# Attention stage: earlier loads, another order on ScalarE, eleven units of maxima, and products on quarters of the array

## The chip, the cores and the metric

The kernel runs on one core of one Trainium2 chip. The metric is device time in microseconds, from the start to the end of one execution, as a median of runs. Of the engines, PE is TensorE's matrix multiplication, PEld its loading of weights, DVE is VectorE, ACT ScalarE, POOL GpSimd and SP SyncE, which here issues the DMAs.

## What is computed

Pooled attention over 4 batches of 8 heads, and behind it two dense layers with a gate. The change touches the attention alone.

```
def _attn_ref(q, k, v):                      # (4, 8, 1152, 64) each, float32
    q_pool = q.reshape(B, H, S // 2, 2, D).mean(axis=3)
    scores = np.matmul(q_pool, k.transpose(0, 1, 3, 2)) / np.sqrt(D)
    scores = scores - np.max(scores, axis=-1, keepdims=True)
    attn = np.exp(scores)
    attn = attn / (np.sum(attn, axis=-1, keepdims=True) + 1e-09)
    return np.matmul(attn, v)

x = attn_out as (2304, 512)
x = (h - tanh(h)) @ w_out            with h = x @ w_in        # first layer
x = (h * sigmoid(1.702 h)) @ w_out   with h = x @ w_in        # second layer
```

## The kernel before

**Stages.** A short preparation, the attention, then the two layers (`moe`). The attention goes by pairs of heads: 16 pairs `p`, one head on partitions 0 to 63 and the other on 64 to 127 (`sides`). A pair has 576 pooled queries (`SP`) and 1,152 keys. It is worked in two halves `x` of 288 queries (`HB`), each over nine tiles of 128 keys: 18 steps `g` per pair, grouped three by three into six *bursts* `c` = 0 to 5. The main loop runs over 96 bursts. Its order is written out by hand, and each engine works through its own instructions in that order; so does SP through its DMAs.

**A burst** issues three times `scores` (L344: four products per head that split q and k into a high and a low part and add the row of maxima; then L347, the exponential on ACT into one of eight buffers `pf`), the units of maxima for the next pair, the additions of probabilities, three times `pv` (L356, v's product, whose two heads lie on the two column halves of the array), and after these a list of `jobs`. `scores` and units share three PSUM slots (`ps`); `acc` and `sm` have one bank each.

**Maxima.** The softmax needs each row's maximum before a pair's scores. `unit` multiplies high parts alone (L292, L300) and DVE reduces the product (L305). There are 14 units per pair: twelve of 2 x 384 columns and two of 2 x 288 for the last 64 queries (the corner). They run in the bursts of the pair before, as 2, 2, 3, 2, 3 in bursts 1 to 5, and the two corners in burst 0 of the pair itself. `max_rows` combines them in two parts, transposes on DVE (L321) and writes rows with six and four small DMAs (L327).

**Sums.** The probabilities are added by two chains: two of three on POOL, the third on DVE (L376). In the next burst 0 or 3 `merge` adds the chains on DVE (L381), and `total` multiplies by ones (L388) and copies to `us` on ACT (L390). `sums` moves one row per head to 128 partitions (L396), `recip` adds the epsilon on POOL (L402), inverts on DVE (L404) and writes to DRAM (L406), `spread` reads it back to all partitions (L412), `normalise` multiplies on DVE (L421).

**Preparation of later pairs.** q and k load at burst 3 of two pairs ahead (L244, L249), k's high part is copied in bursts 4 and 5 on ACT (L277), q's pairs are added on DVE in burst 5 (`qs`, L260), `qh` is copied on ACT in burst 0 (L264), the low parts are subtracted on DVE (L271) and POOL (L284). The loop also loads eight pieces of the layers' weights (L114) and converts each in five steps (L127 to L156), in pairs 3, 4, 6, 7, 9, 10, 12 and 13: the load in burst 0, and one step in each of bursts 1 to 5.

Of the kernel before, what the change touches and what calls it, by code (L numbers as in the profile page):

```python
# [28 lines left out]
def tile_pooled_attention_two_moe(  # L29
# [172 lines left out]
    def attention(ctx: ExitStack):  # L202
# [3 lines left out]
        sides = slice(0, 64), slice(64, 128)  # L206
        KN = S // 3
        QL = SP - 4 * 128
# [8 lines left out]
        sel = ap.tile([128, 128], F32R, name="sel")  # L217
        ones = ap.tile([128, 64], F32, name="ones")
        mts = [[fixed(f"{nm}{i}", 32) for nm in ("mt", "m2", "m3")] for i in range(2)]
# [35 lines left out]
        def have(p, nm, *args):  # L255
            return pairs[p].get(nm) or new(p, nm, *args)

        def prep_qs(p, x=slice(0, SP), eng=nc.vector):
            qs = have(p, "qs", SP, F32, 1)
            eng.tensor_add(qs[:, x], qraw[p][:, 0, x], qraw[p][:, 1, x])  # L260
# [25 lines left out]
        def unit(p, n):  # L286
            d = pairs[p]
            mx = ps.tile([128, 2, 512], F32, tag="ps", name="mx")
            if n < 12:
                j, c = divmod(n, 3)  # L290
                for s, r in enumerate(sides):
                    nc.tensor.matmul(  # L292
                        mx[:, s, 0:KN], d["qh"][r, 128 * j:128 * j + 128],
                        d["kh"][r, KN * c:KN * c + KN], start=True, stop=True)
                at, w = 8 * c + 2 * j, KN
            else:
                a, w = n - 12, HB
# [6 lines left out]
                at = 24 + 2 * a  # L304
            nc.vector.tensor_reduce(  # L305
                d["mt"][:, at:at + 2], mx[:, :, 0:w], AX.X, ALU.max, negate=True)

# [42 lines left out]
        def pv(g):  # L350
            p, i = divmod(g, 2 * KT)
            x, t = divmod(i, KT)
            if t == 0:
                accs[p, x] = ps_acc.tile([128, 512], F32, tag="acc", name="acc")[:, 0:HB]
            for s, r in enumerate(sides):
                nc.tensor.matmul(  # L356
                    accs[p, x][r], pairs[p]["v"][:, s, t, :], probs[g][:, s, :],
                    start=(t == 0), stop=(t == KT - 1))

# [18 lines left out]

        def merge(p, x):
            one, two = parts.pop((p, x, 0))[0], parts[p, x, 1][0]  # L380
            nc.vector.tensor_add(two, two, one)  # L381

        def total(p, x, *more):
            sm = ps_acc.tile([128, 512], F32, tag="sm", name="sm")[:, 0:HB]
            terms = [parts.pop((p, x, 1))[0], *more]
            for n, m in enumerate(terms):
                for s, r in enumerate(sides):
                    nc.tensor.matmul(  # L388
                        sm[r], ones, m[:, s, :], start=(n == 0), stop=(n == len(terms) - 1))
            nc.scalar.activation(results[p][1][:, HB * x:HB * x + HB], sm, AF.Copy)  # L390

        def sums(p):
            us = results[p][1]
            s9 = wpool.tile([128, QJ], F32, tag="s9", name="s9", bufs=2)
            for s, r in enumerate(sides):
                nc.sync.dma_start(  # L396
                    out=s9[r], in_=us[64 * s:64 * s + 1, :].rearrange("o (p i) -> o p i", i=QJ))
            norm[p] = dict(s9=s9)

        def recip(p):  # L400
            r9 = wpool.tile([128, QJ], F32, tag="r9", name="r9", bufs=2)
            nc.gpsimd.tensor_scalar(  # L402
                out=r9, in0=norm[p]["s9"], scalar1=1.0, scalar2=1e-9, op0=ALU.mult, op1=ALU.add)
            nc.vector.reciprocal(r9, r9)  # L404
            rd = drpool.tile([128, QJ], F32, tag="rd", name="rd", bufs=2)
            nc.sync.dma_start(out=rd, in_=r9)  # L406
            norm[p]["rd"] = rd
# [5 lines left out]

        def normalise(p):
            b, hp = divmod(p, NPB)
            t0, done = b * SP, 0
            while done < SP:
                blk = max(x for x in range(NB) if T0S[x] <= t0 + done)
                o = t0 + done - T0S[blk]
                n = min(TBS[blk] - o, SP - done)  # L420
                nc.vector.tensor_mul(  # L421
                    xb[blk][:, hp, o:o + n], results[p][0][:, done:done + n], rbd[:, done:done + n])
                done += n

        NC = 6
        jobs = {}

        def at(p, c, fn, *args):
            jobs.setdefault((p, c), []).append(lambda: fn(*args))

        units = {(0, 0): [(0, 9), (0, 10), (0, 11)], (0, 1): [(0, 12), (0, 13)]}
        for p in range(1, NPAIR):
            n = 0
            for c, m in enumerate((1, 3, 3, 2, 3) if p == 1 else (2, 2, 3, 2, 3), 1):
                units.setdefault((p - 1, c), []).extend((p, n + i) for i in range(m))
                n += m
            units.setdefault((p, 0), []).extend([(p, 12), (p, 13)])
        assert sum(len(u) for u in units.values()) == 14 * NPAIR - 9

        order = (("i", 0), ("i", 1), ("o", 0), ("i", 2), ("i", 3), ("o", 1), ("o", 2), ("o", 3))  # L440
        for p, (kind, f) in zip((3, 4, 6, 7, 9, 10, 12, 13), order, strict=True):
            for c, job in enumerate(piece(kind, f)):
                at(p, c, job)
        for c in range(NKC):
            at(NPAIR - 2 + c // 2, 2 * (c % 2) + 1, split_x, 0, [c], nc.gpsimd)

        for p in range(NPAIR):
            if p > 0:
                at(p - 1, 0, load_v, p)
                at(p - 1, 0, prep_kl, p, 0)  # L450
                at(p - 1, 1, prep_corner, p)
                at(p - 1, 2, prep_ql, p)
                at(p - 1, 3, prep_kl, p, 1)
                at(p, 1, sums, p - 1)
                at(p, 2, recip, p - 1)
                at(p, 3, spread, p - 1)
                at(p, 5, normalise, p - 1)
            if p > 1:
                at(p - 2, 3, load_q, p)
                at(p - 2, 3, load_k, p)  # L460
                at(p - 2, 4, new_pair, p)
                at(p - 2, 4, prep_kh, p, 0)
                at(p - 2, 5, prep_kh, p, 1)
                at(p - 2, 5, prep_qs, p)
                at(p - 1, 0, prep_qh, p)

# [34 lines left out]
        prep_qh(1)  # L501
        for n in range(9):
            unit(0, n)
            keep_warm(3)
        max_rows(0, 0)
        keep_warm(15)

        for c in range(NC * NPAIR):
            p, c = divmod(c, NC)
            x, part = divmod(c, 3)  # L510
            g = p * 2 * KT + 3 * c
            todo = units.get((p, c), [])
            before = (p, 0) if x else (p - 1, 1)
            closing = (p, c) == (NPAIR - 1, NC - 1)
            scores(g)
            for u in todo[:1]:
                unit(*u)
            if part == 0 and before[0] >= 0:
                merge(*before)
            scores(g + 1)  # L520
            scores(g + 2)
            for u in todo[1:]:
                unit(*u)
            if c == 4 and p + 1 < NPAIR:
                max_rows(p + 1, 0)
            if (p, c) == (0, 1) or p > 0 and c == 0:
                max_rows(p, 1)
            if closing:
                merge(p, x)
                add(p, x, 1, 6)  # L530
                add(p, x, 1, 7)
            else:
                for t in (0, 1):
                    add(p, x, 0, 3 * part + t)
# [7 lines left out]
            for job in jobs.pop((p, c), ()):  # L542
                job()
        total(NPAIR - 1, 1, probs[2 * KT * NPAIR - 1])
        sums(NPAIR - 1)
        assert not jobs
        return (lambda: recip(NPAIR - 1), lambda: spread(NPAIR - 1), lambda: normalise(NPAIR - 1))

# [237 lines left out]
```

## Time and profile before

| | us |
|---|---|
| median of 3 runs | 1310.68 (1302.87 to 1314.27) |
| the profiled execution | 1308.84 |
| its span, first to last instruction | 1307.1 |
| PE busy in it | 1236.5 (95%) |
| DVE busy | 974.4 (75%) |
| ACT busy | 633.8 (48%) |
| POOL busy | 475.1 (36%) |

A busy share is an average over the attention and the layers. PE's busy time counts an instruction until its modelled end, so products that overlap leave no gap even where the array streams only part of the time. The starts of instructions are what to compare. A wait is the idle time of an engine ahead of an instruction, put down to whatever released it last.

### The profile page before, as it was taken

To read this page: it belongs to the slowest core of one execution; us is meant where nothing else is said; L and a number is where in the kernel's file an instruction comes from. 1 tells how busy PE (TensorE), PEld (TensorE's weight loads), DVE (VectorE), ACT (ScalarE), POOL (GpSimd) and SP (SyncE) were. 2 spreads that over 40 slices of the span, in tenths; PEclk is the share of its full clock that TensorE was granted. 3 is DMA by queue.
4 is the path that set the end of the run, shared out by engine and by line. 5 is a ranking of instruction groups with operands and counts; after the bars stand their busy time and mean duration, and the time that the engine had idled before them with its cause. 6 is when DMAs were issued, how large, how long until landed. Compare 5 with 4: busy or idle time off the path is not lost.

```text
span 1307.1 us, 20184 instructions
## 1 busy us (share of the span) xinstructions
PE 1236.5 (95%) x7950; PEld 984.5 (75%) x7950; DVE 974.4 (75%) x1190; ACT 633.8 (48%) x944; POOL 475.1 (36%) x329
## 2 busy tenths in 40 slices
PE   8998798888888799999999999999999999999998
PEld 6665555555555567889879889889889889889887
DVE  5877787878888775999999999999943645645433
ACT  3554455444544455777665665665543322322211
POOL 5665565666666664223332332332200100100000
PEclk9999999999999999999999999999999999999999
DMA  3122222212222210111111111101211111111012
GB/s 117 58 101 80 73 74 81 82 65 81 81 65 81 81 29 11 58 36 62 49 33 49 49 33 37 46 33 49 65 33 49 49 33 49 49 33 33 25 41 80
DMA packets 27934, 72.82 MB, mean 56 GB/s; under 512 B 8640, under 2 KB 9152, under 8 KB 27840
## 3 DMA queue, kind: packets, MB, share of 16 engines
q1 hardware_dynamic: 27840, 71.54, 16.7%
q8 instruction: 62, 1.02, 0.3%
q14 instruction: 32, 0.26, 0.1%
HBM read 66.58 MB, written 4.79 MB: 55 GB/s over the span
## 4 chain that ended last, share of the span: by engine, by line
PE 52%; DVE 23%; ACT 8%; DMA 8%; issue 5%; SPq 3%; POOL 1%; DVEq 0%; ACTq 0%; POOLq 0%
PE y L670 21%; PE h L575 20%; PE sc L344 4%; PE acc L356 4%; DVE mt L305 4%; DMA kr<-in_k_dram 3%; DVE gg L633 3%; DVE gg L616 2%; SPq L327 2%; DVE s L376 2%; ACT u L614 2%; ACT pf L347 2%; DVE wt L134 2%; ACT a L635 1%; PE mx L292 1%
## 5 line engine op out<-in xcount | busy, mean ns | idle before, releaser
L305 DVE TENSOR_REDUCE mt<-mx 128x2 fp32r<-128x768 f32 (+1 forms) x224 | 203.4, 923 | 80.2 <-PE mx L292 77.9
L376 POOL TENSOR_TENSOR s<-s,pf 128x576 f32<-128x576 f32 x126 | 179.5, 1425 | 120.2 <-ACT pf L347 115.0
L347 ACT ACTIVATE pf<-sc 128x576 f32<-128x576 f32 x288 | 181.7, 649 | 73.7 <-PE sc L344 70.4
L575 PE MATMUL h<-hl,big 128*128 128x512 f32 (+1 forms) x940 | 211.6, 377 | 0.0
L575 PEld LDWEIGHTS h<-hl,big 128*128 128x128 f32 x940 | 174.0, 188 | 28.5
L156 POOL TENSOR_TENSOR big<-wt,big 128x512 fp32r<-128x512 f32 x46 | 61.5, 1336 | 365.3 <-ACT big L155 365.3
L670 PE MATMUL y<-g,big 128*128 128x512 f32 (+1 forms) x780 | 185.1, 368 | 0.7 <-POOL g L587 0.6
L670 PE MATMUL y<-big,g 128*128 128x512 f32 x702 | 181.0, 390 | 0.0
L356 PE MATMUL acc<-pf,v 128*64 128x288 f32 x1152 | 167.4, 428 | 0.0
L670 PEld LDWEIGHTS y<-g,big 128*128 128x128 f32 x780 | 142.7, 188 | 20.4 <-POOL g L587 1.9
L670 PEld LDWEIGHTS y<-big,g 128*128 128x128 f32 x702 | 131.6, 188 | 27.1
L585 ACT ACTIVATE g<-gg 128x1024 fp32r<-128x1024 f32 (+1 forms) x80 | 78.0, 974 | 137.9 <-DVE gg L646 78.2
L344 PE MATMUL sc<-qh,kh 64*128 64x288 f32 x576 | 104.1, 357 | 35.0 <-ACT pf L347 30.6
L690 DVE TENSOR_TENSOR xb<-xb,y 128x512 f32<-128x512 f32 (+1 forms) x114 | 72.1, 654 | 86.8 <-PE y L670 86.8
L575 PE MATMUL h<-hl,w 128*128 128x512 f32 (+1 forms) x564 | 127.0, 377 | 0.0
L344 PEld LDWEIGHTS sc<-qh,kh 64*128 64x128 f32 x576 | 54.6, 185 | 95.3 <-ACT pf L347 52.8
L356 PEld LDWEIGHTS acc<-pf,v 128*64 128x64 f32 x1152 | 76.3, 141 | 61.5 <-issue 23.9
L575 PEld LDWEIGHTS h<-hl,w 128*128 128x128 f32 x564 | 104.4, 188 | 17.1
L587 POOL TENSOR_TENSOR g<-gg,g 128x1024 fp32r<-128x1024 f32 (+1 forms) x39 | 87.1, 2234 | 65.2 <-ACT g L585 65.2
L635 ACT ACTIVATE a<-u 128x1024 f32<-128x1024 f32 (+1 forms) x40 | 39.1, 977 | 132.0 <-DVE gg L633 132.0
L642 ACT ACTIVATE a<-h 128x1024 f32<-128x1024 f32 (+1 forms) x40 | 37.6, 941 | 117.5 <-PE h L575 117.5
L344 PE MATMUL sc<-row,sel 64*128 64x288 f32 x576 | 86.4, 293 | 1.6 <-issue 1.4
(88 smaller groups left out, 2081.5 us busy)
## 6 DMA issues: line engine op xcount, KB each, us to landing
raw<-in_moe_w_in_dram SPq DMA_DIRECT2D x32, 512.0 KB
raw<-in_moe_w_out_dram SPq DMA_DIRECT2D x32, 512.0 KB
v<-in_v_dram SPq DMA_DIRECT2D x16, 576.0 KB
kr<-in_k_dram SPq DMA_DIRECT2D x15, 576.0 KB
qr<-in_q_dram SPq DMA_DIRECT2D x15, 576.0 KB
rbd<-rd SPq DMA_DIRECT2D x32, 144.0 KB
out_dram<-xb SPq DMA_DIRECT2D x18, 256.0 KB
row<-tt SPq DMA_DIRECT2D x128, 0.5 KB
```

The costliest lines, as they stand in the source:

```text
L156: nc.gpsimd.tensor_tensor(lo, t, f32(hi), op=ALU.subtract)
L305: nc.vector.tensor_reduce(d["mt"][:, at:at + 2], mx[:, :, 0:w], AX.X, ALU.max, negate=True)
L344: nc.tensor.matmul(sc[:, s, 0:HB], w[r], m[r, xs], start=(n == 0), stop=(n == 3))
L347: nc.scalar.activation(pf, sc[:, :, 0:HB], AF.Exp, scale=SCALE)
L356: nc.tensor.matmul(accs[p, x][r], pairs[p]["v"][:, s, t, :], probs[g][:, s, :], start=(t == 0), stop=(t == KT - 1))
L376: eng.tensor_add(out, old, new)
L575: nc.tensor.matmul(hb[:, j, 0:TBS[b]], wi[:, c, w, :], x[r][c], start=(k == 0), stop=(k == 3 * NKC - 1))
L585: nc.scalar.activation(gt[:, :, 0, :], g, AF.Copy)
L587: eng.tensor_tensor(gt[:, :, 1, :], g, f32(gt[:, :, 0, :]), op=ALU.subtract)
L635: nc.scalar.activation(a, u, AF.Relu, bias=-T2)
L670: nc.tensor.matmul(ys[m][:, 0:w], lhsT, rhs, start=(fp == 0 and not low and j == p == 0), stop=(fp == 1 and low and j == 1))
L690: nc.vector.tensor_add(dst, dst, ys[m][:, 0:w])
```

## The change

- The units become eleven: eight of 2 x 512 columns, one (n = 6) that takes the last 128 columns of four query tiles at once, and the two corners. In bursts 1 to 5 they are 2, 2, 2, 1, 2. The first unit of a burst goes behind its second scores.
- `jobs` can be marked `pre`: these are issued ahead of the burst's additions and of v's product, the others behind them as before. The copies `kh`, `qh`, the corner, and the first and last step of a weight piece are `pre`.
- q and k load at burst 0 (two pairs ahead); `qs` is added on POOL at burst 4, in two buffers.
- `pv` and `total` issue four products of 32 output columns, each on its own quarter of the array. `merge` goes: `total` gives the sum of POOL's chain and that of DVE's chain on different quarters, `sums` moves four rows instead of two, and `recip` adds the two and the epsilon in one DVE instruction.
- `normalise` is done in two pieces, one at burst 4 and one at burst 0 of the next pair.
- A weight piece is spread over two pairs, its load in burst 5 ahead of them. `split_x` of the first block goes to pair 15 and from POOL to DVE.

```diff
-        KN = S // 3
+        KN = S - 2 * 512
-            qs = have(p, "qs", SP, F32, 1)
+            qs = have(p, "qs", SP, F32, 2)
 def unit(p, n):
-            if n < 12:
-                j, c = divmod(n, 3)
+            if n == 6:
+                for j in range(4):
+                    for s, r in enumerate(sides):
+                        nc.tensor.matmul(
+                            mx[:, s, KN * j:KN * j + KN], d["qh"][r, 128 * j:128 * j + 128],
+                            d["kh"][r, 2 * 512:], start=True, stop=True)
+                out = d["mt"][:, 16:24].rearrange("p (j s) -> p j s", j=4)
+                src = mx.rearrange("p s (j k) -> p j s k", j=4)
+            elif n < 9:
+                j, c = divmod(n if n < 6 else n - 1, 2)
...
+            nc.vector.tensor_reduce(out, src, AX.X, ALU.max, negate=True)
 def pv(g):
-            for s, r in enumerate(sides):
+            for n in range(4):
+                s, h = divmod(n, 2)
                 nc.tensor.matmul(
-                    accs[p, x][r], pairs[p]["v"][:, s, t, :], probs[g][:, s, :],
-                    start=(t == 0), stop=(t == KT - 1))
+                    accs[p, x][32 * n:32 * n + 32], pairs[p]["v"][:, s, t, 32 * h:32 * h + 32],
+                    probs[g][:, s, :], start=(t == 0), stop=(t == KT - 1))
-        def merge(p, x):
-            one, two = parts.pop((p, x, 0))[0], parts[p, x, 1][0]
-            nc.vector.tensor_add(two, two, one)
 def total(p, x):
+            for n in range(4):
+                s, h = divmod(n, 2)
+                nc.tensor.matmul(
+                    sm[32 * n:32 * n + 32], ones, parts[p, x, h][0][:, s, :], start=True, stop=True)
 def sums(p):
+            for n in range(4):
+                s, h = divmod(n, 2)
                 nc.sync.dma_start(
-                    out=s9[r], in_=us[64 * s:64 * s + 1, :].rearrange("o (p i) -> o p i", i=QJ))
+                    out=s9[sides[s], h, :],
+                    in_=us[32 * n:32 * n + 1, :].rearrange("o (p i) -> o p i", i=QJ))
 def recip(p):
-            nc.gpsimd.tensor_scalar(
-                out=r9, in0=norm[p]["s9"], scalar1=1.0, scalar2=1e-9, op0=ALU.mult, op1=ALU.add)
+            nc.vector.scalar_tensor_tensor(
+                out=r9, in0=s9[:, 0], scalar=1e-9, in1=s9[:, 1], op0=ALU.add, op1=ALU.add)
 the jobs
-        for p, (kind, f) in zip((3, 4, 6, 7, 9, 10, 12, 13), order, strict=True):
+            p = 2 * n + 2
+            when = ((p - 1, 5), (p, 0), (p, 3), (p + 1, 0), (p + 1, 3), (p + 1, 4))
...
+                at(*w, job, pre=n in (1, 5))
-            at(NPAIR - 2 + c // 2, 2 * (c % 2) + 1, split_x, 0, [c], nc.gpsimd)
+            at(NPAIR - 1, 1 + c, split_x, 0, [c], nc.vector)
-                at(p - 1, 1, prep_corner, p)
-                at(p - 1, 2, prep_ql, p)
+                at(p - 1, 1, prep_corner, p, pre=True)
+                at(p - 1, 3, prep_ql, p)
-                at(p, 5, normalise, p - 1)
+                at(p, 4, normalise, p - 1, (0,))
+                if p + 1 < NPAIR:
+                    at(p + 1, 0, normalise, p - 1, (1,))
-                at(p - 2, 3, load_q, p)
-                at(p - 2, 3, load_k, p)
-                at(p - 2, 4, new_pair, p)
-                at(p - 2, 4, prep_kh, p, 0)
-                at(p - 2, 5, prep_kh, p, 1)
-                at(p - 2, 5, prep_qs, p)
-                at(p - 1, 0, prep_qh, p)
+                at(p - 2, 0, load_q, p)
+                at(p - 2, 0, load_k, p)
+                at(p - 2, 4, new_pair, p, pre=True)
+                at(p - 2, 4, prep_kh, p, 0, pre=True)
+                at(p - 2, 5, prep_kh, p, 1, pre=True)
+                at(p - 2, 4, prep_qs, p, slice(0, SP), nc.gpsimd)
+                at(p - 1, 0, prep_qh, p, pre=True)
 the main loop
             scores(g)
+            scores(g + 1)
             for u in todo[:1]:
                 unit(*u)
-            if part == 0 and before[0] >= 0:
-                merge(*before)
-            scores(g + 1)
             scores(g + 2)
             for u in todo[1:]:
                 unit(*u)
+            for job in jobs.pop((p, c, True), ()):
+                job()
...
         total(NPAIR - 1, 1)
```

## Rows read from the trace of the kernel before

**Rows 1.** Windows by pairs: stretch, us, busy PE, PEld, DVE, ACT, POOL; sums over 14, 5, 8
```profile
20.20:46.70 26.50, 26.16 (x264) 17.91 (x262) 20.68 (x30) 14.13 (x25) 17.41 (x12) 1.00 0.18 65
...
482.30:505.50 23.20, 20.95 (x220) 14.16 (x216) 11.73 (x16) 12.68 (x23) 14.90 (x12) 1.00 0.07 15
...
sum 435.60, PE 378.32 PEld 251.31 DVE 350.12 ACT 214.47 POOL 273.68; mean PE 27.02 PEld 17.95 DVE 25.01 ACT 15.32 POOL 19.55
...
sum 146.60, PE 131.41 PEld 87.15 DVE 119.14 ACT 73.51 POOL 100.45; mean PE 26.28 PEld 17.43 DVE 23.83 ACT 14.70 POOL 20.09
...
sum 260.30, PE 220.76 PEld 146.59 DVE 207.74 ACT 126.22 POOL 154.91; mean PE 27.60 PEld 18.32 DVE 25.97 ACT 15.78 POOL 19.36
```

**Rows 2.** Waits in the fourteen inner pairs: who waited for whom, us, times, longest
```profile
PEld sc L344 <- ACT pf L347: 50.9, 70, 3.4
...
ACT kh L277 <- DMA kr<-in_k_dram: 22.9, 13, 3.0
ACT wa L127 <- DMA raw<-in_moe_w_in_dram: 15.2, 4, 4.5
PEld mx L300 <- DVE mt L305: 14.1, 13, 1.4
ACT wa L127 <- DMA raw<-in_moe_w_out_dram: 12.7, 4, 3.6
PEld mx L292 <- DVE mt L305: 12.7, 26, 1.2
...
PEld mx L292 <- ACT qh L264: 8.3, 14, 0.6
```

**Rows 3.** Timeline of PE in pair 2, bursts 2 and 3: start, us, instruction, times
```profile
84.63 0.40 PE L344 MATMUL sc<-qh,kh 64*128 64x288 f32 x2
...
85.26 0.33 PE L292 MATMUL mx<-kh,qh 64*128 64x384 f32 x2
85.44 0.29 PE L344 MATMUL sc<-qh,kh 64*128 64x288 f32 x2
...
86.23 0.40 PE L344 MATMUL sc<-qh,kh 64*128 64x288 f32 x2
...
87.12 1.68 PE L356 MATMUL acc<-pf,v 128*64 128x288 f32 x12
88.73 0.40 PE L344 MATMUL sc<-qh,kh 64*128 64x288 f32 x2
...
92.23 1.68 PE L356 MATMUL acc<-pf,v 128*64 128x288 f32 x12
93.73 0.66 PE L388 MATMUL sm<-s,ones 128*64 128x288 f32 x4
94.32 0.40 PE L344 MATMUL sc<-qh,kh 64*128 64x288 f32 x2
```

**Rows 4.** Groups by line in the fourteen inner pairs: times, busy us, mean ns, idle
```profile
L305 DVE TENSOR_REDUCE mt<-mx 128x2 fp32r<-128x768 f32 x168 | 157.8, 953 | 69.0 <-PE mx L292 68.5
...
L376 POOL TENSOR_TENSOR s<-pf 128x576 f32<-128x576 f32 x28 | 43.8, 1566 | 38.7 <-ACT pf L347 38.3
L381 DVE TENSOR_TENSOR s<-s,s 128x576 f32<-128x576 f32 x28 | 35.3, 1261 | 0.0
...
L305 DVE TENSOR_REDUCE mt<-mx 128x2 fp32r<-128x576 f32 x28 | 20.9, 745 | 0.0
...
L260 DVE TENSOR_TENSOR qs<-qr 128x576 f32<-128x576 f32 x14 | 15.8, 1131 | 0.0
```

**Rows 5.** Timeline: row transfers, a weight load and its use; chain: a k load
```profile
80.61 2.08 SPq L327 DMA_DIRECT2D row<-tt  x4
...
303.32 0.40 SPq L114 DMA_DIRECT2D raw<-in_moe_w_in_dram  x1
...
307.01 0.67 ACT L127 ACTIVATE wa<-raw 128x512 f32<-128x512 f32 x1 [2.99 <-DMA raw<-in_moe_w_in_dram]
...
285.55 5.49 DMA kr<-in_k_dram
```

More of the change, by code (lines that the diff above doesn't have):

```diff
@@ L217, in attention @@
         sel = ap.tile([128, 128], F32R, name="sel")
-        ones = ap.tile([128, 64], F32, name="ones")
+        ones = ap.tile([128, 32], F32, name="ones")
         mts = [[fixed(f"{nm}{i}", 32) for nm in ("mt", "m2", "m3")] for i in range(2)]
@@ L288, in unit @@
             mx = ps.tile([128, 2, 512], F32, tag="ps", name="mx")
-            if n < 12:
-                j, c = divmod(n, 3)
+            a = n - 9
+            if n == 6:
[8 more added lines that the diff above has]
+                j, c = divmod(n if n < 6 else n - 1, 2)
                 for s, r in enumerate(sides):
                     nc.tensor.matmul(
-                        mx[:, s, 0:KN], d["qh"][r, 128 * j:128 * j + 128],
-                        d["kh"][r, KN * c:KN * c + KN], start=True, stop=True)
-                at, w = 8 * c + 2 * j, KN
+                        mx[:, s, :], d["qh"][r, 128 * j:128 * j + 128],
+                        d["kh"][r, 512 * c:512 * c + 512], start=True, stop=True)
+                out, src = d["mt"][:, 8 * c + 2 * j:8 * c + 2 * j + 2], mx
             else:
-                a, w = n - 12, HB
                 for h in range(2):
@@ L303, in unit @@
                             start=(h == 0), stop=(h == 1))
-                at = 24 + 2 * a
-            nc.vector.tensor_reduce(
-                d["mt"][:, at:at + 2], mx[:, :, 0:w], AX.X, ALU.max, negate=True)
+                out, src = d["mt"][:, 24 + 2 * a:26 + 2 * a], mx[:, :, 0:HB]
+            nc.vector.tensor_reduce(out, src, AX.X, ALU.max, negate=True)
         def max_rows(p, part):
@@ L377, in add, with total @@
             parts[key] = out, True
-        def merge(p, x):
-            one, two = parts.pop((p, x, 0))[0], parts[p, x, 1][0]
-            nc.vector.tensor_add(two, two, one)
-        def total(p, x, *more):
+        def total(p, x):
             sm = ps_acc.tile([128, 512], F32, tag="sm", name="sm")[:, 0:HB]
[L385 to L389, printed above, removed]
+            for n in range(4):
+                s, h = divmod(n, 2)
+                nc.tensor.matmul(
+                    sm[32 * n:32 * n + 32], ones, parts[p, x, h][0][:, s, :], start=True, stop=True)
             nc.scalar.activation(results[p][1][:, HB * x:HB * x + HB], sm, AF.Copy)
@@ L393, in sums @@
             us = results[p][1]
-            s9 = wpool.tile([128, QJ], F32, tag="s9", name="s9", bufs=2)
-            for s, r in enumerate(sides):
+            s9 = wpool.tile([128, 2, QJ], F32, tag="s9", name="s9", bufs=2)
+            for n in range(4):
+                s, h = divmod(n, 2)
                 nc.sync.dma_start(
-                    out=s9[r], in_=us[64 * s:64 * s + 1, :].rearrange("o (p i) -> o p i", i=QJ))
+                    out=s9[sides[s], h, :],
+                    in_=us[32 * n:32 * n + 1, :].rearrange("o (p i) -> o p i", i=QJ))
             norm[p] = dict(s9=s9)
         def recip(p):
+            s9 = norm[p]["s9"]
             r9 = wpool.tile([128, QJ], F32, tag="r9", name="r9", bufs=2)
-            nc.gpsimd.tensor_scalar(
-                out=r9, in0=norm[p]["s9"], scalar1=1.0, scalar2=1e-9, op0=ALU.mult, op1=ALU.add)
+            nc.vector.scalar_tensor_tensor(
+                out=r9, in0=s9[:, 0], scalar=1e-9, in1=s9[:, 1], op0=ALU.add, op1=ALU.add)
             nc.vector.reciprocal(r9, r9)
@@ L412, in spread, with normalise @@
                 nc.sync.dma_start(out=rbd[r, 0:SP], in_=row.to_broadcast([64, SP]))
-        def normalise(p):
+        def normalise(p, which=(0, 1)):
             b, hp = divmod(p, NPB)
-            t0, done = b * SP, 0
+            t0, done, pieces = b * SP, 0, []
             while done < SP:
@@ L420, in normalise, with at @@
                 n = min(TBS[blk] - o, SP - done)
+                pieces.append((blk, o, done, n))
+                done += n
+            assert len(pieces) == 2
+            for x in which:
+                blk, o, done, n = pieces[x]
                 nc.vector.tensor_mul(
                     xb[blk][:, hp, o:o + n], results[p][0][:, done:done + n], rbd[:, done:done + n])
-                done += n
         NC = 6
         jobs = {}
-        def at(p, c, fn, *args):
-            jobs.setdefault((p, c), []).append(lambda: fn(*args))
-        units = {(0, 0): [(0, 9), (0, 10), (0, 11)], (0, 1): [(0, 12), (0, 13)]}
+        def at(p, c, fn, *args, pre=False):
+            jobs.setdefault((p, c, pre), []).append(lambda: fn(*args))
+        units = {(0, 0): [(0, 7), (0, 8)], (0, 1): [(0, 9), (0, 10)]}
         for p in range(1, NPAIR):
             n = 0
-            for c, m in enumerate((1, 3, 3, 2, 3) if p == 1 else (2, 2, 3, 2, 3), 1):
+            for c, m in enumerate((1, 2, 2, 2, 2) if p == 1 else (2, 2, 2, 1, 2), 1):
                 units.setdefault((p - 1, c), []).extend((p, n + i) for i in range(m))
                 n += m
-            units.setdefault((p, 0), []).extend([(p, 12), (p, 13)])
-        assert sum(len(u) for u in units.values()) == 14 * NPAIR - 9
+            units.setdefault((p, 0), []).extend([(p, 9), (p, 10)])
+        assert sum(len(u) for u in units.values()) == 11 * NPAIR - 7
         order = (("i", 0), ("i", 1), ("o", 0), ("i", 2), ("i", 3), ("o", 1), ("o", 2), ("o", 3))
-        for p, (kind, f) in zip((3, 4, 6, 7, 9, 10, 12, 13), order, strict=True):
-            for c, job in enumerate(piece(kind, f)):
-                at(p, c, job)
+        for n, (kind, f) in enumerate(order):
+            p = 2 * n + 2
+            when = ((p - 1, 5), (p, 0), (p, 3), (p + 1, 0), (p + 1, 3), (p + 1, 4))
+            if n == 6:
+                when = ((13, 5), (14, 0), (14, 3), (15, 0), (15, 1), (15, 2))
+            elif n == 7:
+                when = ((14, 1), (15, 1), (15, 2), (15, 3), (15, 4), (15, 5))
+            for n, (w, job) in enumerate(zip(when, piece(kind, f), strict=True)):
+                at(*w, job, pre=n in (1, 5))
         for c in range(NKC):
-            at(NPAIR - 2 + c // 2, 2 * (c % 2) + 1, split_x, 0, [c], nc.gpsimd)
+            at(NPAIR - 1, 1 + c, split_x, 0, [c], nc.vector)
         for p in range(NPAIR):
@@ L501, in attention @@
         prep_qh(1)
-        for n in range(9):
+        for n in range(7):
             unit(0, n)
-            keep_warm(3)
+            keep_warm(4)
         max_rows(0, 0)
@@ L527, in attention @@
                 max_rows(p, 1)
[L528 to L534, printed above, removed]
+            for t in (0, 1):
+                add(p, x, int(closing), 3 * part + t)
+            if not closing:
                 add(p, x, 1, 3 * part + 2)
@@ L541, in attention @@
                 take(p, x)
-            for job in jobs.pop((p, c), ()):
+            for job in jobs.pop((p, c, False), ()):
                 job()
-        total(NPAIR - 1, 1, probs[2 * KT * NPAIR - 1])
+        add(NPAIR - 1, 1, 1, KT - 1)
+        total(NPAIR - 1, 1)
         sums(NPAIR - 1)
         assert not jobs
-        return (lambda: recip(NPAIR - 1), lambda: spread(NPAIR - 1), lambda: normalise(NPAIR - 1))
+        return (
+            lambda: (normalise(NPAIR - 2, (1,)), recip(NPAIR - 1)),
+            lambda: spread(NPAIR - 1), lambda: normalise(NPAIR - 1))
     def moe(ctx: ExitStack, ending):
```

## The prediction

> **What bounds the kernel now.** Read the windows by head pair first [rows 1]. The changed stage is 485.3 us of the span: pair 0 (26.5), fourteen inner pairs (435.6, mean 31.1) and pair 15, which has no successor to prepare (23.2). About 20 us lie ahead of it and 801.6 us behind it; the change touches those only at their edges. In the inner pairs TensorE is recorded busy for 27.0 us a pair, VectorE 25.0, GpSimd 19.6, ScalarE 15.3: no engine is full, so the stage is set by engines waiting for each other. The five pairs without weight pieces beyond pair 1 take 146.6 / 5 = 29.3 us, the eight with one take 260.3 / 8 = 32.5 us.
>
> Then read the PE timeline of one burst in which nothing is late [rows 3]. It starts at 84.63 and the next one at 88.73: 4.10 us, with two units of maxima. A set of scores takes 0.52 us there (four times 0.13), a 384-column unit 85.44 - 85.26 = 0.18. The second scores, begun at 85.44, are through at 85.96, but the third start at 86.23, when the first exponential has freed a PSUM slot; that 0.27 us is the one wait that stays. Six v products' slots last 93.73 - 92.23 = 1.50 us, so two products side by side take 0.25 us. A burst with a chain of sums behind it spends 94.32 - 92.23 = 2.09 us from v's product to the next scores instead of 88.73 - 87.12 = 1.61, so a total costs 0.48 us. Twelve inner units of 384 columns and two corners then make a pair of 6 x 4.10 + 2 x 0.18 (third units) + 2 x 0.48 + 0.07 (corners) = 26.0 us. Pair 0 takes 26.5, near that floor; the inner pairs take 31.1.
>
> The list of waits says what fills the 5.1 us between [rows 2]: PE's weight loads for scores wait 50.9 us for exponentials (3.6 a pair, of which six times 0.27 = 1.6 is the wait inside the floor), for reductions of maxima 14.1 + 12.7 (1.9 a pair), for the copy qh 8.3 (0.6). Those make 4.5 us; the rest is restart and clock. The exponentials are late because ScalarE, which works in order, stands at a copy whose load has not landed: 22.9 us at kh and 15.2 + 12.7 us at the weights' first step.
>
> **Loads and ScalarE's order.** k and q now load in burst 0 for a use in burst 4, not in burst 3. A k load issued behind q lands 5.49 us after its issue [rows 5]; behind v as well I add about 2.3 us (half of the 5.49, which held two such loads, less start-up), 7.8 us, against some 13 us of lead. The 22.9 us go. A weight piece issues behind the six row transfers of burst 4: at 0.52 us each (2.08 / 4, rows 5) they end some 2.6 us into burst 5, and its first step stands behind the third exponential of the next burst, 4.7 us later; the load takes 307.01 - 303.32 = 3.7 us. The 27.9 us go as well, with 1 us to spare; without that cover the 3.5 us per piece come back. With qh ahead of the copy `us` its 0.6 us a pair goes. What ScalarE does in all stays near 15.3 us a pair [rows 1], 58% of the new period.
>
> **VectorE.** Removed per pair: two merges at 1.261 and qs at 1.131 [rows 4], 3.65 us. Units: 768 columns cost 953 ns and 576 cost 745, that is 1.083 ns a column, so 1,024 cost 953 + 256 x 1.083 = 1,230 ns; nine of them are 11.07 us where twelve were 11.44. Added: the sum of the two halves of s9 with the epsilon, 128 x 18, between nothing and one contended add (1.26); I take 0.3. So VectorE falls from 25.0 to about 21.3 us, 3.55 us a burst against 4.2 of PE. The steps of a weight piece are spread over bursts 0 and 3, where no unit-heavy add stands. splits of x leave POOL for VectorE in pair 15 alone, which has no maxima (11.73 us busy of 23.2): nothing.
>
> **GpSimd.** qs arrives, at about the 1,566 ns that a first add takes there [rows 4], and the first step of the reciprocal leaves: at most 19.6 + 1.6 = 21.2 us of 26.6. It may run one burst late, since eight probability buffers hold more than two bursts. If it is later than that, the total on PE waits for it directly, as the merge did.
>
> **TensorE.** The units stream the same columns (12 x 768 = 8 x 1,024 + 1,024). v's product and the totals become four products of 32 output columns where two of 64 stood, each streaming the same 288 columns [rows 3]. No row shows a quarter. If four run side by side a slot stays 0.25 us and the change costs nothing; if they go two by two it is 0.50 us. Bounds: 0 and 0.25 us for each of 40 slots a pair (18 x 2 + 2 x 2), 0 to 10 us. I take nothing, since the nearest row, two halves, shows products on different columns sharing one slot (12 in 1.50 us, where one alone streams at least as long), and each quarter has its own columns as each half has.
> The Trainium skill, TensorE: Matmul & The Clock Gate, Part 3, speaks partly against this: three column tiles measured 2.38 times one, not 3. An estimate by that ratio is 0.25 x 3 / 2.38 = 0.315 us a slot, 2.6 us a pair, and a time near 1,287 us; no run here shows it yet.
>
> **The sum.** A burst with two wide units: 4.10 + 0.06 (a 512-column unit for a 384-column one; the first hides in the wait before the third scores) = 4.16 [rows 3]. Bursts 0 to 5: 4.71 (two corners, a total), 4.16, 4.16, 4.64 (a total), 3.94 (one unit), 4.16: 25.8 us. On top I put 0.8: pair 0 runs 0.5 over its floor, and VectorE is 83% full. 26.6 x 14 = 372.4, for 435.6: -63.2. Pair 0: 26.5 to 25.4, -1.1. Pair 15 takes in two pieces and four splits but loses merges: 0. The end: the last sum goes through one more VectorE add in place of four products, +0.7. Start: 7 wide units for 9, with four fillers for three, 0 (0.3 either way). Together -63.6. The profiled execution took 1308.84 (span 1307.1 and 1.7 around it), 1.8 under the median of 1310.68, so **1245 us**.
>
> **Rivals.**
> *Late sums on VectorE (chance 0.16).* The reciprocal's first step leaves GpSimd for VectorE, and waits there for s9, with the next reductions queued behind it and PE behind those. SP now issues v, q and k ahead of the four s9 transfers. Corner maxima end about 4.4 us into a pair, four row transfers 2.1 us later [rows 5], k some 1.2 us after that, and k lands 7.8 us on: s9 comes at about 15.5 us. VectorE reaches the step at about 13.7, after bursts 0 to 2 (13.0). That 1.8 us wait delays the next reduction to 17.1, and its slot is wanted at 17.7: hidden by 0.6. Each us later is lost: with 2 to 2.5 us more the period is about 28.4 and the time 1245 + 14 x 1.8 = 1270 us (1262 to 1276). For it: nothing in the trace has s9 behind three loads. Against: the two row transfers' times leave slack.
> *Quarters in turn (0.10).* Four quarters two by two: 10 us more a pair on an engine that sets the period, 1245 + 16 x 10 = 1405 us. It decides from 63.6 / (16 x 40) = 0.10 us a slot, that is 0.35 us. For it: no quarter in the trace. Against: halves don't take turns.
> *Quarters in part (0.07).* A slot between 0.29 and 0.37: 1270 to 1320 us (0.03 of it faster, 0.03 the same, 0.01 slower).
> *No residue (0.07).* The floor of 25.8 is reached: 1245 - 14 x 0.8 = 1234 us or somewhat less.
> The change not doing what it says would be q's load held at SP by qs on a late GpSimd, with k behind it; with 5 us of lead to spare I count it inside the first rival.
>
> **How the numbers follow.** Forecast 0.60, at 1236 to 1256 us of its own. The range 1230 to 1282 takes in the late sums and nearly all of the floor, and leaves out the quarters' cases, about 0.17. One per cent is 13 us, what a measurement of this kernel can tell from no change. Faster by more: 0.60 + 0.16 + 0.07 + 0.03 = 0.86; the same 0.03; slower 0.10 + 0.01 = 0.11.
>
> **What would show it.** Twelve-slot rows of v's product: 24 products in about 1.5 us (right) or 3 us (quarters in turn). The waits of kh and the weights' first step on loads: near nothing. A VectorE wait for a transfer at the new reciprocal step, and its length. Merges and qs gone from VectorE, its busy time per pair near 21 us. Inner pairs near 26.6 us, with weight pairs no longer than others. The forecast is wrong if PE still waits over 1 us a pair for maxima, or if a slot of v's product leaves 0.25 us.

## The result and the profile after

The changed kernel takes 1265.66 us (median of 4 runs, 1263.65 to 1267.59) beside 1311.33 for the kernel before on the same chip: a ratio of 0.966 (0.961 to 0.971), 3.4% faster. The forecast was 1245, with a range of 1230 to 1282. The profiled execution took 1263.65 with a span of 1261.9, which divides as follows (us of the span, stages by the first exponential of a pair).

| stage | before | after | difference | forecast |
|---|---|---|---|---|
| start | 20.2 | 19.8 | -0.4 | 0 |
| pair 0 | 26.5 | 25.9 | -0.6 | -1.1 |
| fourteen inner pairs | 435.6 | 382.5 | -53.1 | -63.2 |
| pair 15 and the end of the attention | 26.2 | 26.4 | +0.2 | +0.7 |
| the two layers | 798.6 | 807.3 | +8.7 | 0 |
| span | 1307.1 | 1261.9 | -45.2 | -63.6 |

So 18.4 us of the forecast are missing: 10.1 in the inner pairs, 8.7 in the layers, whose code was not touched. Windows after, of the inner pairs and of the layers (stretch, us, busy PE, PEld, DVE, ACT, POOL, granted clock, DMA share, GB/s); [rows 1] has the inner pairs of before:

```profile
45.76:428.24 382.48, 363.00 (x4710) 234.93 (x4708) 340.95 (x390) 211.14 (x376) 279.20 (x188) 1.00 0.26 86
454.61:1261.90 807.29, 800.75 (x3747) 686.29 (x3744) 579.55 (x660) 387.14 (x508) 160.85 (x95) 1.00 0.12 43
```

An inner pair takes 27.3 us. VectorE is busy for 340.95 / 14 = 24.4 us of it, not the 21.3 forecast, and GpSimd for 19.9. The waits after, in the same stretch (who for whom, us, times, longest):

```profile
PEld sc L351 <- DVE mt L313: 38.2, 51, 2.5
DVE r L408 <- DMA s<-us: 27.6, 14, 4.1
PEld sc L351 <- ACT pf L354: 24.0, 70, 0.7
PEld sm L391 <- POOL s L384: 6.2, 6, 1.5
```

Against [rows 2] the waits for kh, for raw weights and for qh are gone, and the wait for exponentials fell from 50.9 to 24.0, which is 1.7 a pair: the 1.6 that the prediction put inside the floor. What is new is a VectorE wait of 27.6 us for the small transfers s9 (the sums of a pair, moved to 128 partitions) at the step that came from GpSimd, in every pair, and with it PE's 38.2 us for reductions of maxima. The chain can be followed in pair 7, the pair that lost most. Timeline after of SP, VectorE and PE (start, us, instruction, times, the idle time before it and what ended that):

```profile
211.13 2.09 SPq L334 DMA_DIRECT2D row<-tt  x4
213.33 0.34 SPq L253 DMA_DIRECT2D v<-in_v_dram  x1
214.10 0.33 SPq L244 DMA_DIRECT2D qr<-in_q_dram  x1
214.49 0.42 SPq L249 DMA_DIRECT2D kr<-in_k_dram  x1
215.01 4.20 SPq L400 DMA_DIRECT2D s<-us  x4
...
223.82 0.17 DVE L408 SCALAR_TENSOR_TENSOR r<-s 128x9 f32<-128x9 f32 x1 [4.09 <-DMA s<-us]
224.03 0.22 DVE L410 RECIPROCAL r<-r 128x9 f32<-128x9 f32 x1
224.16 2.29 DVE L313 TENSOR_REDUCE mt<-mx 128x2 fp32r<-128x1024 f32 x2
...
225.38 0.40 PE L351 MATMUL sc<-qh,kh 64*128 64x288 f32 x2 [1.94 <-DVE mt L313]
...
228.15 2.78 PE L364 MATMUL acc<-pf,v 128*32 128x288 f32 x24
230.86 0.40 PE L351 MATMUL sc<-qh,kh 64*128 64x288 f32 x2
```

SP issues v, q and k and then s9; s9 lands at 223.8. VectorE stands at it for 4.09 us, the two reductions queued behind it begin at 224.16, and PE, whose next scores need one of the three PSUM slots, stands for 1.94 us. The windows that follow show a second price: in the first PE is busy for 2.06 of 4 us, and behind it the granted clock falls from 1.00 to 0.76 and 0.59, that is toward the 1.2 GHz level, and v's product takes 2.78 us there instead of 1.66:

```profile
222.00:226.00 4.00, 2.06 (x32) 1.14 (x26) 2.14 (x4) 0.41 (x1) 1.67 (x2) 1.00 0.05 5
226.00:228.00 2.00, 2.00 (x28) 1.83 (x24) 2.00 (x4) 1.24 (x2) 0.00 (x0) 0.76 0.26 84
228.00:231.00 3.00, 3.00 (x28) 1.11 (x28) 2.93 (x5) 1.74 (x3) 1.44 (x1) 0.59 0.16 48
```

In most pairs the wait is shorter and cheaper. In pair 1 it is 1.73 us, burst 3 takes 4.93 us where 4.6 is what it takes without a wait, and v's product has its forecast length (24 products in 61.94 - 60.46 = 1.48 us, up to the total behind it):

```profile
53.67 2.53 SPq L400 DMA_DIRECT2D s<-us  x4
...
60.64 0.85 DVE L408 SCALAR_TENSOR_TENSOR r<-s 128x9 f32<-128x9 f32 x1 [1.73 <-DMA s<-us]
...
60.46 1.66 PE L364 MATMUL acc<-pf,v 128*32 128x288 f32 x24
61.94 0.67 PE L391 MATMUL sm<-s,ones 128*32 128x288 f32 x8
```

### The profile page after: what moved, and what is told of

It is laid out like the page before. It is cut to its first block, busy times and chain, and to the rows that moved or that the text cites. A ratio compares the mean times of both kernels' runs of the same rounds, so it can differ in the third digit from the quotient of the medians.

```text
span 1261.9 us, 22678 instructions
## 1 busy us (share of the span) xinstructions
PE 1229.8 (97%) x9228; PEld 966.5 (77%) x9228; DVE 972.5 (77%) x1117; ACT 632.2 (50%) x944; POOL 483.1 (38%) x323
## 4 chain that ended last, share of the span: by engine, by line
PE 52%; DVE 24%; ACT 7%; DMA 5%; SPq 4%; issue 4%; POOL 4%; DVEq 0%; ACTq 0%; POOLq 0%
PE y L687 21%; PE h L592 20%; PE sc L351 5%; DMA s<-us 5%; DVE mt L313 5%; PE acc L364 3%; POOL s L384 3%; DVE gg L650 3%; DVE gg L633 2%; DVE wt L134 2%; ACT u L631 2%; SPq L400 2%; ACT a L652 1%; DVE wt L128 1%; DVE xb L707 1%
## 5 line engine op out<-in xcount | busy, mean ns | idle before, releaser
L354 ACT ACTIVATE pf<-sc 128x576 f32<-128x576 f32 x288 | 177.8, 650 | 123.6 <-PE sc L351 122.5
L384 POOL TENSOR_TENSOR s<-s,pf 128x576 f32<-128x576 f32 x126 | 192.7, 1529 | 54.5 <-ACT pf L354 49.6
L313 DVE TENSOR_REDUCE mt<-mx 128x2 fp32r<-128x1024 f32 (+2 forms) x176 | 192.6, 1128 | 23.4 <-PE mx L301 16.2
L687 PE MATMUL y<-big,g 128*128 128x512 f32 x702 | 185.1, 395 | 0.0
L364 PE MATMUL acc<-pf,v 128*32 128x288 f32 x2304 | 160.7, 412 | 0.0
L592 PEld LDWEIGHTS h<-hl,w 128*128 128x128 f32 x564 | 104.5, 188 | 18.4
L364 PEld LDWEIGHTS acc<-pf,v 128*32 128x32 f32 x2304 | 65.1, 110 | 64.7 <-issue 20.7
```

The costliest lines, as they stand in the source:

```text
L313: nc.vector.tensor_reduce(out, src, AX.X, ALU.max, negate=True)
L354: nc.scalar.activation(pf, sc[:, :, 0:HB], AF.Exp, scale=SCALE)
L364: nc.tensor.matmul(accs[p, x][32 * n:32 * n + 32], pairs[p]["v"][:, s, t, 32 * h:32 * h + 32], probs[g][:, s, :], start=(t == 0), stop=(t ...
L384: eng.tensor_add(out, old, new)
L592: nc.tensor.matmul(hb[:, j, 0:TBS[b]], wi[:, c, w, :], x[r][c], start=(k == 0), stop=(k == 3 * NKC - 1))
L687: nc.tensor.matmul(ys[m][:, 0:w], lhsT, rhs, start=(fp == 0 and not low and j == p == 0), stop=(fp == 1 and low and j == 1))
```

## The experiments

Each kernel differs from the changed one (called *after*) by its edit alone, unless it says otherwise. Theory: the late sums cost the inner pairs, and what the layers lost comes from where the buffers lie. Rivals: VectorE is simply too full, GpSimd is too late for the totals, or the layers' loss is chance.

**loads_behind_sums** puts the loads of q and k behind the four s9 transfers.

```diff
-                at(p - 2, 0, load_q, p)
-                at(p - 2, 0, load_k, p)
+                at(p - 2, 1, load_q, p)
+                at(p - 2, 1, load_k, p)
```


> The changed kernel with the loads of q and k in burst 1, behind the four small transfers of the sums, instead of ahead of them. Theory 'late sums': VectorE's wait of 27.6 us for those transfers (2 us a pair) falls under 5 us; as VectorE and that wait fill 26.3 of the 27.3 us of an inner pair, the pair falls to about 26.2 us and the time by 12 to 16 us. Rival 'absorbed': the wait goes but only the bursts where it was seen to delay scores gain, 0.3 us in most and 1.5 us in three pairs, 6 to 8 us in all.

**after_again**, the changed kernel once more, ran beside it.

> The changed kernel itself, once more. In its first trace the attention ended 53.9 us earlier than before, but the span was only 45.2 us shorter: in the two layers, whose code is the same, 512-column products follow each other every 229 to 233 ns where they took 227. Theory 'addresses' (the layers' buffers lie 64 bytes further on, off a 128-byte line): the same again, 229 in the first layer and 233 in the second, about 1264 us. Rival 'that execution' (something of the chip or the run): near 227 in both layers, and about 1256 us.

Measured: 1249.49 us (ratio to before 0.952, 0.950 to 0.954) beside 1261.53 (0.961, 0.959 to 0.963): 12.0 us for the order of the loads. The waits of after_again are close to those of after (25.6 us for s9, 34.4 for reductions). Windows and waits of loads_behind_sums in the inner pairs:

```profile
45.89:413.49 367.60, 358.89 (x4709) 233.63 (x4708) 343.91 (x390) 211.42 (x376) 275.23 (x187) 1.00 0.29 90
...
PEld sc L351 <- DVE mt L313: 17.3, 37, 0.5
PEld sm L391 <- POOL s L384: 8.9, 6, 1.7
DVE r L408 <- DMA s<-us: 0.5, 1, 0.5
```

The wait for s9 falls from 27.6 to 0.5 us and PE's wait for reductions from 38.2 to 17.3, while VectorE is as busy as in after (343.91). The odd pairs take 25.75 us (pair 1 25.84), in bursts of 4.62, 4.21, 4.20, 4.60, 3.93 and 4.19 (starts of the exponentials); the prediction's floor was 4.71, 4.16, 4.16, 4.64, 3.94 and 4.16. So the late sums are the cause, and a full VectorE is not. The six even pairs from 4 on take 26.8 to 27.1: in burst 0 PE's total waits for a GpSimd addition, as the 8.9 us show.

**before_gap64** and **after_gap64** ask after the layers. In after, s9 has two buffers of 72 bytes per partition where it had 36; laid out in steps of 32 bytes, that moves every buffer of the layers that is laid out behind it by 64 bytes. Each kernel gets an unused 64 bytes ahead of the layers' buffers (before_gap64 is the kernel before with it):

```diff
     rbd = wpool.tile([128, 2 * TB], F32, name="rbd")
+    wpool.tile([128, 16], F32, name="gap")
```


> The kernel before with the 64 bytes, so that its layers' operands lie where those of the changed kernel lie. Theory 'addresses': 229 and 233 ns between products, the layers 8 to 9 us longer, about 1319 us, 0.6% slower than before. Rival 'that execution': no difference (within 4 us of 1311).

> The changed kernel with 64 unused bytes ahead of the buffers, so that the layers' operands lie on the same 128-byte lines as before. Theory 'addresses': 227 ns between 512-column products in both layers, the layers 8 to 9 us shorter, about 1256 us. Rival 'that execution': no difference from the changed kernel beyond noise (1262 to 1268 us), whatever the spacing is. The attention is the same for both (inner pairs near 27.3 us).

Measured: 1320.19 us for before_gap64 (1.005, 1.003 to 1.007) and 1265.69 for after_gap64 (0.964, 0.962 to 0.967). Windows of the layers, first of before_gap64, then of after_gap64 (before has 508.46 to 1307.10, 798.64 us):

```profile
511.78:1318.70 806.92, 800.91 (x3746) 686.74 (x3744) 579.17 (x658) 387.28 (x508) 161.77 (x96) 1.00 0.13 43
```
```profile
455.20:1266.60 811.40, 806.79 (x3747) 691.59 (x3744) 579.55 (x660) 387.52 (x508) 159.64 (x95) 1.00 0.13 43
```

64 unused bytes alone make the layers of the kernel before 8.3 us longer. The version of the theory by which another 64 bytes would bring after back (a rule of 128 bytes) fell: the layers got 4.1 us longer still.

**same_lines** gives every buffer of the layers the address that it has in before, **lines_and_loads** is same_lines and loads_behind_sums together:

```diff
+    wpool.tile([128, 8], F32, name="gap")
...
-            s9 = wpool.tile([128, 2, QJ], F32, tag="s9", name="s9", bufs=2)
+            s9 = wpool.tile([128, 2, QJ], F32, tag="s9", name="s9")
```


> The changed kernel with one buffer of s9 instead of two and 32 unused bytes, so that every buffer of the two layers lies at the very address that it has in the kernel before. Theory 'addresses': 227 ns between 512-column products in both layers as before, the layers near 799 us instead of 807, the time near 1254 us. Rival 'what ran ahead' (the layers are slower because of the attention ahead of them, or only the offset of 64 bytes mattered by chance): 229 and 233 ns again, about 1262 us.

> Both together: the layers at the addresses of the kernel before, and the loads of q and k behind the transfers of the sums. If the two effects are independent, 1249.5 - 8.5 = 1241 us, 0.946 of the kernel before; if the wait for the sums comes back with a single s9 buffer, about 1254 us.

Measured: 1251.29 us (0.956, 0.954 to 0.958) and **1242.65** (0.948, 0.946 to 0.950), the fastest kernel of the study. The layers of same_lines, and then a group of the second layer in before, after and same_lines (times, busy us, mean ns of one):

```profile
449.70:1248.90 799.20, 792.13 (x3747) 686.30 (x3744) 580.65 (x660) 387.46 (x508) 159.66 (x95) 1.00 0.13 44
```
```profile
L670 PE MATMUL y<-big,g 128*128 128x512 f32 x702 | 181.0, 390 | 0.0
```
```profile
L687 PE MATMUL y<-big,g 128*128 128x512 f32 x702 | 185.1, 395 | 0.0
```
```profile
L688 PE MATMUL y<-big,g 128*128 128x512 f32 x702 | 181.0, 390 | 0.0
```

The same 702 products take 390 ns at the old addresses and 395 at the new ones. That the addresses set the layers' time is shown; why is open.

**qs_vector** is lines_and_loads with qs back on VectorE, against GpSimd's lateness.

```diff
-                at(p - 2, 4, prep_qs, p, slice(0, SP), nc.gpsimd)
+                at(p - 2, 5, prep_qs, p)
```


> The kernel of the last run with the addition qs back on VectorE in burst 5, as in the kernel before. Even pairs still lose 1.1 us in burst 0 (5.7 against 4.62 us), where the total on TensorE waits for GpSimd's chain. Theory 'GpSimd is late' (the split of a weight piece and qs both stand in burst 4): without qs the wait goes, six to seven pairs gain about 1.1 us, and VectorE's blocked additions get shorter too: 6 to 8 us less, about 1234 us. Rival 'VectorE has no room': the 0.75 us and what GpSimd holds back of it put reductions late in burst 5, each pair loses 0.3 us or more, and the time is the same or up to 6 us longer.

Measured: 1244.57 us (0.951, 0.948 to 0.953), not faster. Burst 0 of the even pairs from 4 on takes 4.7 to 4.85 us where it took 5.7 to 6.0, but burst 1 takes 5.3 to 7.1 where it took 4.2. In pair 6 VectorE works from qs at 177.83 without a pause, and comes to the wide reduction of burst 1 at 187.09, 4.4 us into that burst:

```profile
PEld sc L352 <- DVE mt L314: 31.3, 42, 2.9
...
177.83 1.97 DVE L261 TENSOR_TENSOR qs<-qr 128x576 f32<-128x576 f32 x1
...
187.09 1.21 DVE L314 TENSOR_REDUCE mt<-mx 128x2 fp32r<-128x1024 f32 x1
```

The other kernels undo one part of the change each, to size it.

**loads_late** loads q and k at burst 3 again (`at(p - 2, 3, load_q, p)` and the same for k).

> The changed kernel with one part undone: q and k load in burst 3 again, instead of burst 0. Theory 'the loads carried much of the gain': ScalarE waits for k at the copy kh again, and earlier than in the kernel before since the copy now stands ahead of v's product; 2 us or more in each of 14 pairs, less the 12 us that the late sums cost (they are free of the two loads now): 1270 to 1290 us. Rival 'the loads were hidden anyway': the waits at kh stay short, and with the sums on time the time falls to about 1250 us.

Measured: 1276.88 us (0.974, 0.971 to 0.977), 27 more than loads_behind_sums, with which it shares sums that land in time. Its waits in the inner pairs:

```profile
PEld sc L351 <- ACT pf L354: 49.6, 69, 3.9
ACT kh L277 <- DMA kr<-in_k_dram: 36.9, 13, 4.7
DVE r L408 <- DMA s<-us: 0.2, 1, 0.2
```

**no_pre** issues every job behind the burst (`pre = False`).

> The changed kernel with one part undone: every prepared step behind the burst's additions and v's product again, none ahead. Theory: the copy qh comes late again for the first unit of burst 1 (0.6 us a pair, 8 us in all) and the two copies of kh push the first exponential of the next burst (up to 0.7 us each); 1270 to 1285 us. Rival 'hidden': the first unit now stands behind the second scores, 0.5 us later, so qh is in time anyway; within 4 us of 1264.

Measured: 1261.41 us (0.961, 0.959 to 0.963), the same as after. PE's wait for qh is back, but at 4.5 us in all where [rows 2] has 8.3; the first unit now stands behind the second scores, which may be why. The time does not move. VectorE still waits 21.9 us for s9 in this kernel, and the order was not tried where the sums are in time.

**merge_back** takes back v's product and the totals on halves, the merge on VectorE (behind the first unit), two s9 transfers, and the reciprocal's first step on GpSimd:

```diff
-            for n in range(4):
-                s, h = divmod(n, 2)
+            for s, r in enumerate(sides):
                 nc.tensor.matmul(
-                    accs[p, x][32 * n:32 * n + 32], pairs[p]["v"][:, s, t, 32 * h:32 * h + 32],
-                    probs[g][:, s, :], start=(t == 0), stop=(t == KT - 1))
+                    accs[p, x][r], pairs[p]["v"][:, s, t, :], probs[g][:, s, :],
+                    start=(t == 0), stop=(t == KT - 1))
...
+        def merge(p, x):
+            one, two = parts[p, x, 0][0], parts[p, x, 1][0]
+            nc.vector.tensor_add(two, two, one)
...
-            nc.vector.scalar_tensor_tensor(
-                out=r9, in0=s9[:, 0], scalar=1e-9, in1=s9[:, 1], op0=ALU.add, op1=ALU.add)
+            nc.gpsimd.tensor_scalar(
+                out=r9, in0=s9[:, 0], scalar1=1.0, scalar2=1e-9, op0=ALU.mult, op1=ALU.add)
```


> The changed kernel with one part undone: v's product and the totals on halves of the array, the two chains merged on VectorE again, two transfers for the sums and the first step of the reciprocal on GpSimd. Theory 'VectorE sets the pair': two merges of 1.26 us more, less 2 us of waiting for s9, which moves to GpSimd; about +0.5 to +1 us a pair, 1270 to 1280 us. Rival 'the quarters brought nothing but the late sums': 1250 to 1258 us. The slot of v's product stays 0.25 us with either.

Measured: 1289.21 us (0.983, 0.980 to 0.986), 24 to 28 more than after. Waits:

```profile
PEld sm L393 <- DVE s L388: 38.5, 28, 3.4
POOL r L408 <- DMA s<-us: 26.4, 13, 3.7
DVE r L410 <- POOL r L408: 21.4, 13, 3.4
DVE s L388 <- POOL s L383: 15.9, 6, 2.8
```

The late transfer is still late: here GpSimd waits for it, and VectorE for GpSimd. PE's total stands behind the merge in all 28 cases. The inner pairs take 398.9 us, 16 to 20 more than in after and after_again (382.5 and 378.9); the rest of the loss lies outside them. Most of it stands in burst 0 of the six even pairs from 4 on, where the merge itself waits for GpSimd: 7.7 to 8.8 us, 16.2 us more than these six bursts take in after.

**units14** has the fourteen units of before again (three in bursts 3 and 5), **units14_behind** the same with the loads behind the sums:

```diff
-        KN = S - 2 * 512
+        KN = S // 3
...
-            for c, m in enumerate((1, 2, 2, 2, 2) if p == 1 else (2, 2, 2, 1, 2), 1):
+            for c, m in enumerate((1, 3, 3, 2, 3) if p == 1 else (2, 2, 3, 2, 3), 1):
```


> The changed kernel with one part undone: 14 units of maxima per pair again (three in bursts 3 and 5) instead of 11. By the two floors the units are worth 26.0 - 25.8 = 0.2 us a pair on TensorE, 3 us in all; theory 'VectorE sets the pair': three more reductions' fixed cost, 14 x 0.95 against 11 x 1.2, 0.4 us a pair, and more where three stand in one burst: 1268 to 1276 us. Rival 'free': within 3 us of 1264.

> 14 units of maxima as in the run before (1327 us), with the loads of q and k behind the transfers of the sums. In that run burst 3 took 7 to 11 us, since its third unit waits for a PSUM slot that VectorE frees only after its wait for s9, and v's product stands behind that unit. Theory 'the third unit exposes the late sums': with the sums on time burst 3 falls to about 5 us, and the time to 1250 to 1262 us. Rival 'three units in a burst are dear in themselves': burst 3 stays over 6 us and the time over 1285 us.

Measured: 1327.48 us (1.011, 1.007 to 1.016), 1.1% above the kernel before, and 1274.33 (0.972, 0.969 to 0.975), between the two forecasts. Timeline of units14 in pair 7, VectorE and PE, and its waits:

```profile
256.67 0.82 DVE L401 SCALAR_TENSOR_TENSOR r<-s 128x9 f32<-128x9 f32 x1 [1.71 <-DMA s<-us]
257.65 2.64 DVE L305 TENSOR_REDUCE mt<-mx 128x2 fp32r<-128x768 f32 x3
...
258.61 0.69 PE L292 MATMUL mx<-kh,qh 64*128 64x384 f32 x2 [2.12 <-DVE mt L305]
259.22 2.84 PE L357 MATMUL acc<-pf,v 128*32 128x288 f32 x24
...
PEld mx L292 <- DVE mt L305: 58.6, 28, 4.8
DVE r L401 <- DMA s<-us: 31.3, 14, 4.7
```

The third unit of burst 3 needs a PSUM slot; the slot waits for a reduction, the reduction for s9, and v's product stands behind the unit. Burst 3 takes 7.1 to 11.2 us in thirteen of the fourteen inner pairs. With the sums in time (wait 0.9 us) it falls to 4.9 to 5.2, but burst 5, which also has three units, still takes 5.5 to 7.7 in those thirteen instead of 4.2, and PE waits 22.9 us for slots, most of it there. So the units are worth 25 us with sums in time, and 62 to 66 where sums are late. Part of the latter is the clock: 24 products take 2.84 us above, and the mean granted clock of the run is 0.979 where after has 0.998.

## Why the prediction was right and where it was short

The result lies in the range, 20.7 us above the forecast. With the late sums and the moved buffers both undone (lines_and_loads) the change takes 1242.65, where the forecast without either term was 1245. By the prediction's own sign, over 1 us a pair of PE waiting for maxima, the forecast was wrong: 38.2 / 14 = 2.7.

**The floor** of 25.8 us was right: 25.75 in the odd pairs of loads_behind_sums. The forecast's 0.8 of residue was near, 26.26 on the mean there, which leaves 0.5, though its source was another: GpSimd's additions ahead of the totals, 1.1 to 1.3 us in six even pairs (in after four of them show it), not VectorE.

**Loads ahead** was right. The waits left the list, and loads_late prices them at 27 us.

**Quarters** were right at a slot of 0.25 us: 24 products in 1.48 us; both rivals on them fell. The prediction's estimate of 0.315 us a slot, worked out from the ratio of 2.38 for three column tiles in the Trainium skill, TensorE: Matmul & The Clock Gate, Part 3, does not agree with this row, and the measurement decides. What the quarters let go is the merge. merge_back puts it, with what belongs to it, at 24 to 28 us, of which 1.2 to 1.4 a pair in the inner pairs. VectorE is no busier there (337.6 us for 340.95), so the price lies in the wait of PE's total rather than in VectorE's load, and most of it falls where GpSimd is late as well. The prediction had booked merges as VectorE's load alone.

**The term that failed most: late sums.** The prediction had the place and the mechanism as a rival with a chance of 0.16 and counted them at nothing in the sum. It put the step at 13.7 us into a pair, s9 at 15.5, the next reduction at 17.1. In pair 1, which begins at 45.76, the step is reached at 13.2 (60.64 - 1.73), goes at 14.9, and the reduction at 15.9. The wait was sized right, 27.6 / 14 = 2.0 for 1.8; "hidden by 0.6" was the wrong step. It supposed that 1.8 us of lateness fit between VectorE and PE, and did not ask how the wait varies: in pair 1 the four s9 transfers were issued in 2.53 us and the wait was 1.73, in pair 7 in 4.20 and it was 4.09. The time that the rival gave, 1270 (1262 to 1276), holds the result, but partly by luck: its price was 12 us and not 25, and the layers, which no rival had, added 8.7.

**VectorE at 21.3 us** failed: 24.4. Groups by line in the inner pairs, first before, then after (times, busy us, mean ns):

```profile
L317 DVE TENSOR_TENSOR m<-mt 128x2 fp32r<-128x2 f32 x14 | 8.0, 575 | 0.0
L318 DVE TENSOR_TENSOR m<-m 64x2 fp32r<-64x2 f32 x14 | 3.4, 240 | 0.5
L421 DVE TENSOR_TENSOR xb<-u,rbd 128x320 f32<-128x320 f32 x8 | 4.9, 617 | 0.0
```
```profile
L313 DVE TENSOR_REDUCE mt<-mx 128x2 fp32r<-128x1024 f32 x112 | 130.8, 1209 | 7.8 <-PE mx L301 7.6
L324 DVE TENSOR_TENSOR m<-mt 128x2 fp32r<-128x2 f32 x14 | 14.0, 1002 | 0.0
L325 DVE TENSOR_TENSOR m<-m 64x2 fp32r<-64x2 f32 x14 | 13.7, 981 | 0.5
L432 DVE TENSOR_TENSOR xb<-u,rbd 128x320 f32<-128x320 f32 x8 | 10.8, 1346 | 0.0
```

The reductions, which read PSUM, came as worked out (1,209 ns for 1,230). Operations with two inputs in SBUF got longer, a two-column one from 240 to 981 ns on the mean. Its spread (ns, shortest/median/longest), before and after, shows two lengths:

```profile
L318 DVE TENSOR_TENSOR m<-m x14: 155/156/1333, 49.9 to 458.6; 64x2 fp32r<-64x2 f32 x14
L325 DVE TENSOR_TENSOR m<-m x14: 155/1268/1345, 48.6 to 405.7; 64x2 fp32r<-64x2 f32 x14
```

In both traces it takes 155 to 157 ns where no GpSimd instruction runs beside it, 13 times of 14 before and 4 after, and 1,261 to 1,345 where one is already running when it starts, ending 14 to 20 ns after that instruction. This agrees with the Trainium skill, SBUF — State Buffer, Who interferes with whom: a VectorE instruction with two SBUF inputs contends with a GpSimd instruction that reads SBUF, and the order of issue decides which of them blocks. Taking durations over from a trace in which such operations fell beside GpSimd's less often was the error; GpSimd is busy for 73% of an inner pair after, 63% before. It cost little: at 24.6 us busy the odd pairs of loads_behind_sums run at the floor.

**Units** were mis-sized. They were booked as 0.4 us of VectorE a pair and two shapes of burst; units14_behind shows 25 us. A third unit in a burst makes v's product wait for a reduction; the prediction listed 1.9 us a pair of waits for maxima but did not lay them to the third unit. The prices of undone parts do not add up: 27 for the loads, 25 for the units and 24 to 28 for merge_back are more than the whole gain of 46 to 50. **The order on ScalarE**, booked at 0.6 us a pair, is worth nothing that can be measured where the sums are late (no_pre).

**The layers** were "touched only at their edges". The 8.7 us of their loss are a term that no row of before could show; same_lines gives them back (799.2 us).

**The clock** was no term either. The inner pairs of before have a granted clock of 0.98, between 13 and 22 us of 435.6 at 1.2 GHz by the rounding of that row; those of after have 1.00. Some of the gain lies there; how much was not separated from the stalls themselves.

## What to carry to other kernels

Before a waiting step is moved to another engine that works in order, list what is queued behind it there, and issue the small transfer that it waits for ahead of the large ones on the same queue: here that order alone was worth 12 us. Durations from a trace hold for the overlap in that trace; an operation whose neighbours change needs its own bound. When a buffer's size changes, compare the products of untouched stages before and after, since everything laid out behind it moves.

## What was not expected of the hardware

The rate of the layers' products depends on where in SBUF the buffers lie. The median distance between the starts of successive 512-column products is 227 ns in both layers of before, same_lines, lines_and_loads and qs_vector; 229 in the first and 233 in the second layer in after, before_gap64 and the other kernels that lie 64 bytes further on; and 232 to 233 in both in after_gap64, 128 bytes further on. The granted clock is 1.00 in all of them. Of the products' operands only the activations (`hl`, `g`) lie behind the added bytes; the weights' buffers come ahead of them in the kernel and did not move. Which of these buffers matters, and why, was not separated.
